# Attention and a gated feed-forward: the sum of e over the partitions by accumulating transfers

## The chip, the core and the metric

The kernel runs on one core of a Trainium2 chip. Its time is the device time of one execution in microseconds (us), the median of three runs. The engines of the core work side by side, each with its own queue of instructions in a fixed order, and wait for each other by semaphores: TensorE (PE) multiplies matrices, ScalarE (ACT) evaluates functions, VectorE (DVE) does elementwise work and sums, GpSimd (POOL) here issues transfers and clears a few tiles, and SyncE (SP) issues transfers. A transfer is issued from an engine's queue and carried out by 16 DMA engines that all queues share.

## The reference

Thirty-two heads (4 batches of 8) of 768 queries and keys, 64 numbers each. Queries and keys are hashed to six bits; a query sees only keys of its own bucket. The result, laid out as 3072 rows of 512, passes through a gated feed-forward with 2048 hidden columns.

```
q_bits = (einsum(q, proj) > 0); k_bits likewise          # 6 bits each
mask   = bucket(q)[..., :, None] == bucket(k)[..., None, :]
scores = where(mask, q @ k.T / sqrt(64), -1e9)
e      = exp(scores - max(scores))
x      = (e / (sum(e) + 1e-9)) @ v                       # to (3072, 512)
h      = x @ w_in
out    = (h * erf(softplus(h))) @ w_out
```

## The kernel before

Heads are worked two at a time: 16 pairs. In a pair each half of the queries (384 of 768) is a step h, so there are 32. Scores are held transposed, with 128 keys on the partitions and queries along the row, in six blocks per step for both heads of the pair: TensorE writes a block (`score`, L548), which adds a product of hash bits that pushes foreign buckets down and the product of q and k; ScalarE takes the exponential into `e_all` (L566), a ring of nine blocks; TensorE multiplies with v (`weigh`, L629).

The softmax needs, for every query, the sum of e over all keys. VectorE adds the six blocks of a step to one of 128 x 768 (`sum_keys`, L617). What remains is a sum over the 128 partitions. `divisor` (L664) does it on TensorE by four products with a block of ones; `keep_divisor` (L677) copies the result from PSUM. When both steps of a pair are there, `spread` and `gather` (L707, L714) take the 1536 sums through DRAM to 128 partitions, `invert` (L724 to L727) takes reciprocals, and `ungather`, `widen` (L732, L742) bring them back, repeated over 64 partitions. `normalise` (L750) multiplies, `send` stores x to DRAM.

Beside that the weights come in. They arrive as 64-bit numbers in 32 pieces of 128 x 512 (`fetch_weights`, L454, from GpSimd's queue but for the first two). VectorE and ScalarE turn each into 32 bits: `square_high` and `keep_normal` on ScalarE, `move_bits` (two instructions), `mask_bits` (two) and `add_rest` (two) on VectorE. In `add_rest` one instruction makes the rest from the low word (L522) and a second adds it to the top (L530). `presum_weights` (L771) forms sums of weight blocks that the feed-forward uses in place of some products.

GpSimd's queue also carries the hash bits of the pair after next: `leave_bits` (L846) writes signs to DRAM, `place_bits` (L855, two transfers) brings them to the rows where TensorE reads them. The second waits for the first to land, and the scores of that pair wait for both.

The order of all this is made by a planner, `arrange`: each operation has an engine, a cost, a rank, a list of operations that it follows, and `late`, the time after its end until another engine can use its result. The planner plays this through and writes each engine's instructions in the order it finds; on the chip each engine then keeps that order and waits where data are not there. In the planner `late` counts between engines only:

```
away = 0.0 if names[a].engine == op.engine else names[a].late     # L141
```

Attention and feed-forward are planned apart; the last pair's divisor is finished inside the feed-forward (`late`). The feed-forward works six blocks of 512 rows; it has transfers from GpSimd's queue that add to what stands in SBUF (`accum_op`, L1372), fifteen in all.

Of the kernel before, what the change touches and what calls it, by code (L numbers as in the profile page):

```python
# [193 lines left out]
def kernel(  # L194
# [219 lines left out]
    def attention():  # L414
        NS = NPAIR * 4
        with (
# [10 lines left out]
            def big(name):  # L427
# [49 lines left out]
            def move_bits(n):  # L477
                if n not in raws:
                    return
                high = raws[n][:, :, 1]  # L480
                top = raws[n, "top"] = cvt.tile([P, WP], I32, name="top", tag="top")
                nc.vector.tensor_scalar(
                    out=top,
                    in0=high,
                    scalar1=3,
                    scalar2=0x7FFFFFFF,
                    op0=ALU.logical_shift_left,
                    op1=ALU.bitwise_and,
                )
                nc.vector.scalar_tensor_tensor(  # L490
                    out=top,
                    in0=high,
                    scalar=SIGN,
                    in1=top,
                    op0=ALU.bitwise_and,
                    op1=ALU.bitwise_or,
                )

            def mask_bits(n):
                if n not in raws:  # L500
                    return
# [13 lines left out]

            def add_rest(n):
                if n not in raws:
                    return
                top, unit = raws.pop((n, "top")), raws.pop((n, "unit"))
                low = raws.pop(n)[:, :, 0]  # L520
                rest = cvt.tile([P, WP], F32, name="rest", tag="rest")
                nc.vector.scalar_tensor_tensor(  # L522
                    out=rest,
                    in0=low.bitcast(U32),
                    scalar=2.0**-52,
                    in1=unit[:, :].bitcast(F32),
                    op0=ALU.mult,
                    op1=ALU.mult,
                )
# [63 lines left out]
            def sum_keys(h, k):  # L593
                i, half = divmod(h, 2)
                d = pairs[i]
                if k == 0:
                    if h >= NH - 2:
                        if half:
                            room = blocks[1][:, :, :].rearrange("p k t -> p (k t)")[:, 0:S]
                        else:  # L600
                            room = load.tile([P, S], F32, name="q", tag="q")
                        d["sum", half] = room.rearrange("p (n a c) -> p n a c", n=1, a=2)
                    else:
                        d["sum", half] = wide_sums[h % 2]
                s = d["sum", half]
# [9 lines left out]

                into = s[:, 0:2, :, :] if where == 2 else s[:, where : where + 1, :, :]
                nc.vector.tensor_tensor(out=into, in0=term(one), in1=term(two), op=ALU.add)  # L617

# [18 lines left out]
            def home(i, what):  # L637

                if i < NPAIR - 1:
                    shape, bufs = {"x": (S, 3), "z": (HS, 1), "r": (S, 2)}[what]  # L640
                    return xst.tile([P, shape], F32, name=what, tag=what, bufs=bufs)
                rows = blocks[1][:, :, :].rearrange("p k t -> p (k t)")
# [47 lines left out]
            def leave_plain(i):  # L690
# [9 lines left out]
                )  # L700

            def spread(i):

# [25 lines left out]
            def ungather(i):  # L729
                d = pairs[i]  # L730
                rd = d["rd"] = dram.tile([2, 2, HS], F32, name="rd", tag="rd")
                nc.sync.dma_start(  # L732
                    out=rd.rearrange("h a c -> (h a c)").rearrange("(p c) -> p c", c=2 * S // P),
                    in_=d["zc"],
# [144 lines left out]
            for h in range(NH):  # L879
# [3 lines left out]
                if h % 2 and (h + 3) // 2 < NPAIR:  # L883
                    order.append(("bits", (h + 3) // 2))
                if h >= 1:
                    order.append(("divisor", h - 1))
                order += [("weigh", 2 * h), ("weigh", 2 * h + 1)]
            slots = []
            for what, n in order:
# [12 lines left out]
                else:  # L902
                    h = n // 2
                    after = (("exponential", n, GC - 1),)
                    if n % 2 == 0:
                        after += (("leave", h - 1), ("leave_plain", (h - 1) // 2))
                    pe(weigh, (n,), 2.02, after)
            sums_after = {}
            for h in range(NH):
# [16 lines left out]
            for h in range(NH):  # L926
                for k, (blocks_, _, _, where) in enumerate(sum_steps(h)):
                    after = tuple(("exponential", 2 * h + b // GC, b % GC) for b in blocks_)
                    after += (("sum_keys", h, k - 1), ("sum_keys", h - 1, last_sum(h - 1)))
                    if k == 0:  # L930
                        after += (("divisor", h - 2),)
# [13 lines left out]
            for h in range(NH):  # L945
                i = h // 2
                op(leave, (h,), "ACT", 0.48, (0, 2 * h, -2), (("weigh", 2 * h + 1), ("send", i - 3)))
                if h % 2 == 0:
                    op(leave_plain, (i,), "DVE", 0.15, (0, 2 * h, 0), (("weigh", 2 * h + 1),))
            for i in range(NPAIR):  # L950
# [40 lines left out]
                if i == NPAIR - 1:  # L991
                    continue
                op(spread, (i,), "SP", 0.4, (0, n, 0), (("keep_divisor", 2 * i + 1),), late=3.0)
                op(gather, (i,), "SP", 0.35, (0, n, 1), (("spread", i),), late=4.5)
                op(invert, (i,), "DVE", 0.4, (0, n + 8, 3), (("gather", i),))
                op(ungather, (i,), "SP", 0.35, (0, n, 2), (("invert", i),), late=3.0)
                op(
# [12 lines left out]
            for n in range(len(pieces)):  # L1010
# [13 lines left out]
                op(mask_bits, (n,), "DVE", 1.1, (2, n, 1), (("move_bits", n), ("keep_normal", n)), late=1.5)  # L1024
                op(add_rest, (n,), "DVE", 1.3, (2, n, 2), (("mask_bits", n),))
            for k in range(8):
                op(
                    presum_weights,
                    (k,),
                    "DVE",  # L1030
                    1.2,
                    (2, 31, k),
                    (("add_rest", 8 * (k // 4) + 7), ("presum_weights", k - 1)),
                )
            op(load_x, (0,), "SP", 1.1, (1, 0), (("send", JP - 1), ("start_pair", 10)), late=4.0)
# [748 lines left out]
```

## Time and profile before

| | |
|---|---|
| median of three runs | 911.17 us (909.92 to 911.47) |
| the profiled execution, its own time | 910.96 us |
| span of its trace, first to last instruction | 909.2 us |
| attention, to TensorE's first product of the feed-forward | 321.6 us |
| TensorE busy | 900.3 us |
| VectorE, ScalarE, GpSimd busy | 673.3, 571.9, 58.2 us |
| TensorE clock granted in the span (mean) | 0.999 |
| records of products with ones (L664) | 256, 0.33 us each, eight to a divisor |

Busy times of an engine are sums of its instructions; where one engine is busy all the time, the others' idle time costs nothing. In rows of instructions the first numbers are the start in the span and the duration, then engine, line, operation, and written tile <- read tiles with their shapes; brackets hold the idle time before an instruction and what ended it. A row of transfers holds their count, the size of one and the time from issue to landing. In rows by stretch of time the columns are PE, weight loads, DVE, ACT, POOL busy time, then the granted clock, the share of the DMA engines and GB/s.

### The profile page before, as it was taken

What the parts mean: (1) busy time and instruction counts of PE and PEld (TensorE: products, weight loads), DVE (VectorE), ACT (ScalarE), POOL (GpSimd) and SP (SyncE); (2) the same over time, 40 slices, a digit from 0 to 9 for tenths busy, and PEclk for the clock granted to TensorE, in tenths of its full rate; (3) what the DMA queues carried; (4) which work ended last, traced back from release to release, by engine and by line L of the source; (5) the groups of instructions that cost most, each with busy time, mean ns of one, the idle gap of its engine ahead of it and who ended that gap; (6) DMA issues with size and microseconds to landing.
All of it is one profiled execution on the core that took longest, in us unless ns stands there. A gap on an engine that the chain in (4) does not pass through costs nothing.

```text
span 909.2 us, 12885 instructions
## 1 busy us (share of the span) xinstructions
PE 900.3 (99%) x5016; PEld 661.9 (73%) x5016; DVE 673.3 (74%) x863; ACT 571.9 (63%) x824; POOL 58.2 (6%) x95
## 2 busy tenths in 40 slices
PE   9999999999999999999999999999999999999997
PEld 5444444444444478888888888888888888888886
DVE  5989999989999969986566556756776556655653
ACT  6878887888887849755555545555655555545520
POOL 0211111111121000000000001000100000000000
PEclk9999999999999999999999999999999999999999
DMA  8455677656574231111122114211321023101321
GB/s 203 130 162 148 169 176 189 187 141 165 157 194 136 59 123 64 38 45 70 52 65 82 35 47 105 81 36 47 87 99 35 35 58 94 35 32 52 69 70 50
DMA packets 65013, 86.83 MB, mean 96 GB/s; under 512 B 34348, under 2 KB 47500, under 8 KB 64944
## 3 DMA queue, kind: packets, MB, share of 16 engines
q1 hardware_dynamic: 56384, 63.81, 24.6%
q0 software_dynamic: 8112, 21.66, 8.6%
q8 instruction: 41, 0.67, 0.3%
q10 hardware_dynamic: 448, 0.46, 0.2%
q14 instruction: 28, 0.23, 0.1%
HBM read 64.67 MB, written 17.30 MB: 90 GB/s over the span
## 4 chain that ended last, share of the span: by engine, by line
PE 92%; issue 1%; DMA 1%; ACT 0%; POOL 0%; DVE 0%; DVEq 0%; ACTq 0%; POOLq 0%
PE M L1317 32%; PE X L1204 28%; PE st L548 14%; PE av L629 12%; PE M L1204 3%; PE z_ps L664 1%; PE bits L817 1%; DMA raw<-in_w_in_dram 0%; POOL both L855 0%; ACT e_all L566 0%; ACT keep L468 0%; DMA bd<-sg 0%; DVE u L1352 0%; ACT x L688 0%; DVEq L1727 0%
## 5 line engine op out<-in xcount | busy, mean ns | idle before, releaser
L1244 DVE SCALAR_TENSOR_TENSOR e<-w,e 128x1024 f32<-128x1024 f32 x144 | 173.8, 1221 | 8.9 <-ACT w L1238 4.2
L566 ACT ACTIVATE e_all<-st 128x768 f32<-128x768 f32 x192 | 150.9, 813 | 11.9 <-PE st L548 11.5
L1238 ACT ACTIVATE w<-h,cq 128x1024 f32<-128x1024 f32 x144 | 155.6, 1137 | 0.2 <-DVE e L1244 0.2
L548 PE MATMUL st<-q,k 64*128 64x384 f32 x768 | 155.0, 483 | 0.0
L1226 DVE TENSOR_TENSOR h<-X,h 128x512 f32<-128x512 f32 x65 | 44.8, 689 | 146.0 <-PE X L1204 145.8
L1317 PE MATMUL M<-w_out_sb,h 128*128 128x256 f32 x576 | 141.5, 379 | 0.0
L629 PE MATMUL av<-e_all,v 128*64 128x385 f32 (+1 forms) x768 | 131.1, 490 | 0.0
L1204 PE MATMUL X<-x,w_in_sb 128*128 128x256 f32 x512 | 121.0, 379 | 0.0
L1317 PEld LDWEIGHTS M<-w_out_sb,h 128*128 128x128 f32 x576 | 109.4, 190 | 14.9
L1222 ACT COPY h<-X 128x512 f32<-128x512 f32 x85 | 49.3, 580 | 112.4 <-PE X L1204 112.3
L1234 ACT ACTIVATE e<-h,cq 128x1024 f32<-128x1024 f32 x48 | 55.2, 1150 | 82.7 <-DVE h L1226 82.7
L1204 PEld LDWEIGHTS X<-x,w_in_sb 128*128 128x128 f32 x512 | 97.3, 190 | 13.2
L629 PEld LDWEIGHTS av<-e_all,v 128*64 128x64 f32 x768 | 52.4, 136 | 67.2 <-issue 65.2
L1317 PE MATMUL M<-wt,S 128*128 128x256 f32 x384 | 95.6, 379 | 0.0
L548 PEld LDWEIGHTS st<-q,k 64*128 64x128 f32 x768 | 68.2, 188 | 34.9 <-issue 34.2
L1204 PE MATMUL X<-x_sum,w_sum 128*128 128x256 f32 x344 | 81.3, 379 | 0.0
L1317 PEld LDWEIGHTS M<-wt,S 128*128 128x128 f32 x384 | 73.0, 190 | 9.9
L1204 PEld LDWEIGHTS X<-x_sum,w_sum 128*128 128x128 f32 x344 | 65.4, 190 | 8.9
L548 PE MATMUL st<-both 64*128 64x384 bf16 x384 | 62.9, 324 | 1.6 <-ACT e_all L566 1.4
L1259 DVE TENSOR_TENSOR h<-h,e 128x1024 f32<-128x1024 f32 x48 | 58.0, 1221 | 3.7 <-ACT e L1255 3.6
L1255 ACT ACTIVATE e<-e 128x1024 f32<-128x1024 f32 x48 | 50.4, 1054 | 7.8 <-DVE e L1244 7.4
L548 PEld LDWEIGHTS <-both 64*128 64x128 bf16 x384 | 19.5, 94 | 43.1 <-issue 21.2
(126 smaller groups left out, 1073.4 us busy)
## 6 DMA issues: line engine op xcount, KB each, us to landing
wt<-wt SPq DMA_DIRECT2D x24, 768.0 KB, 4.2
raw<-in_w_out_dram POOLq DMA_DIRECT2D x16, 512.0 KB, 4.6
raw<-in_w_in_dram POOLq DMA_DIRECT2D x14, 512.0 KB, 4.3
v<-in_v_dram SPq DMA_DIRECT2D x32, 192.0 KB, 4.8
xs<-x SPq DMA_DIRECT2D x16, 384.0 KB, 3.1
q<-in_qkT_dram SPq DMA_DIRECT2D x30, 192.0 KB, 4.2
k<-in_qkT_dram SPq DMA_DIRECT2D x30, 192.0 KB, 4.4
r<-rd SPq DMA_DIRECT2D x30, 192.0 KB, 3.4
```

Source lines behind the costliest of these rows:

```text
L548: nc.tensor.matmul(out=st[:, ab, 0:HS], lhsT=d["k" + src][rows, keys], rhs=d["q" + src][rows, cols], start=(part == 0), stop=(part == 1),)
L566: nc.scalar.activation(out=e[:, :, 0:HS], in_=st[:, :, 0:HS], func=AF.Exp, scale=scale)
L629: nc.tensor.matmul(out=d["av"][rows, 0:w], lhsT=d["v"][:, g * GC + c, rows], rhs=e[:, ab, 0:w], start=(g == 0 and c == 0), stop=(g == 1 an ...
L1204: nc.tensor.matmul(out=d[where][:, u, :], lhsT=a[:, kc, f : f + P], rhs=b[:, kc, :], start=(first and u == 0 and kc == 0), stop=(last and ...
L1222: nc.scalar.copy(out=quarter(p, q), in_=st[p][where])
L1226: nc.vector.tensor_tensor(out=h, in0=st[p][where], in1=h, op=ALU.add)
L1234: nc.scalar.activation(out=s, in_=unit(p, v), func=AF.Sigmoid, bias=cq[:, n : n + 1])
L1238: nc.scalar.activation(out=q, in_=unit(p, v), func=AF.Sigmoid, scale=GATE_S[j][0], bias=cq[:, j : j + 1])
L1244: nc.vector.scalar_tensor_tensor(out=s, in0=st[p].pop(("q", v, j)), scalar=GATE_S[j][2], in1=s, op0=ALU.add, op1=ALU.mult,)
L1255: nc.scalar.activation(out=s, in_=s, func=AF.Tanh, scale=GATE_LEAD)
L1259: nc.vector.tensor_tensor(out=h, in0=h, in1=st[p].pop(("s", v)), op=ALU.mult)
L1317: nc.tensor.matmul(out=banks[name][:, sub, :], lhsT=a[:, u, sub * P : (sub + 1) * P], rhs=b[:, u, :], start=(c == 0 and k == 0), stop=(c = ...
```

## The change

For 14 of the 16 pairs (`FOLDED`) the products with ones and their copies are left out. The last addition of `sum_keys` writes its 128 x 768 into half of a row block of 128 x 1536 that holds both steps of the pair (`pair_sums`, two of them, used in turn). Four transfers from GpSimd's queue then add the lower half of the rows to the upper: 64 rows to 64, 32 to 32, 16 to 16, 8 to 8 (`fold`). Eight rows go to DRAM and come back as 64 partitions x 8 x 24; VectorE adds the eight and inverts. The last two pairs keep the old form.

For the weights, the second instruction of `add_rest` is replaced by an accumulating transfer of 128 x 512 (`complete_weights`): the top is formed where the weights will lie, and the rest is added there. `unit` gets two buffers; the order of `presum_weights` is new, with two of them after the last use of `w_sum` as a row block. `x` has four buffers in place of three.

```diff
+    FOLDS = 4
+            FOLDED = NPAIR - 2
+            pair_sums = [
+                t.rearrange("p a b -> p (a b)")[:, 0 : 2 * S]
+                for t in (blocks[1][:, :, :], w_sum[:, 2, :, :])
+            ]
...
-                top = raws[n, "top"] = cvt.tile([P, WP], I32, name="top", tag="top")
+                top = raws[n, "top"] = pieces[n][0].bitcast(I32)
...
-                unit = raws[n, "unit"] = cvt.tile([P, WP], I32, name="unit", tag="unit")
+                unit = raws[n, "unit"] = cvt.tile([P, WP], I32, name="unit", tag="unit", bufs=2)
...
-                nc.vector.tensor_tensor(
-                    out=pieces[n][0], in0=top[:, :].bitcast(F32), in1=rest, op=ALU.add
+
+            def complete_weights(n):
+
+                if (n, "unit") not in raws:
+                    return
+                nc.gpsimd.dma_start(
+                    out=pieces[n][0],
+                    in_=raws.pop((n, "unit"))[:, :].bitcast(F32),
+                    accum_op=ALU.add,
                 )
...
+                if i < FOLDED and k == last_sum(h):
+                    into = pair_sums[i % 2][:, half * S : (half + 1) * S].rearrange(
+                        "p (n a c) -> p n a c", n=1, a=2
+                    )
...
+            def fold(i, k):
+
+                n = P >> (k + 1)
+                s = pair_sums[i % 2]
+                nc.gpsimd.dma_start(out=s[0:n, :], in_=s[n : 2 * n, :], accum_op=ALU.add)
+
+            ROWS = P >> FOLDS
+
+            def spread_folded(i):
+
+                zf = pairs[i]["zf"] = dram.tile([ROWS, 2 * S], F32, name="zf", tag="zf")
+                nc.sync.dma_start(out=zf, in_=pair_sums[i % 2][0:ROWS, :])
+
+            def gather_folded(i):
+                d = pairs[i]
+                zr = d["zr"] = small.tile([D, ROWS, 2 * S // D], F32, name="zr", tag="zr", bufs=2)
+                nc.sync.dma_start(
+                    out=zr, in_=d.pop("zf").rearrange("r (p c) -> p r c", c=2 * S // D)
+                )
+
+            def invert_folded(i):
+                d = pairs[i]
+                zc = d["zc"] = small.tile([D, 2 * S // D], F32, name="zc2", tag="zc2")
+                nc.vector.tensor_reduce(
+                    out=zc, in_=d.pop("zr").rearrange("p r c -> p c r"), axis=AX.X, op=ALU.add
+                )
+                nc.vector.tensor_scalar(
+                    out=zc, in0=zc, scalar1=S * EPS, scalar2=None, op0=ALU.add
+                )
+                nc.vector.reciprocal(out=zc, in_=zc)
...
-                if h >= 1:
+                if h - 1 >= 2 * FOLDED:
                     order.append(("divisor", h - 1))
...
+                    if k == last_sum(h) and i_of(h) < FOLDED:
+                        after += (("spread_folded", i_of(h) - 2),)
...
-            for h in range(NH - 1):
+            for h in range(2 * FOLDED, NH - 1):
...
+                if i < FOLDED:
+                    for k in range(FOLDS):
+                        before = ("fold", i, k - 1) if k else ("sum_keys", 2 * i + 1, last_sum(2 * i + 1))
+                        op(fold, (i, k), "POOL", 0.9, (0, n, 4 + k), (before,), late=4.0)
+                    op(spread_folded, (i,), "SP", 0.4, (0, n, 0), (("fold", i, FOLDS - 1),), late=3.0)
+                    op(gather_folded, (i,), "SP", 0.35, (0, n, 1), (("spread_folded", i),), late=4.5)
+                    inverse = invert_folded
+                    op(inverse, (i,), "DVE", 0.7, (0, n + 8, 3), (("gather_folded", i),))
...
-                op(add_rest, (n,), "DVE", 1.3, (2, n, 2), (("mask_bits", n),))
...
+                op(add_rest, (n,), "DVE", 0.7, (2, n, 2), (("mask_bits", n), ("complete_weights", n - 2)))
+                op(complete_weights, (n,), "POOL", 0.9, (0, n, 1), (("add_rest", n),), late=4.5)
```

More of the change, by code (lines that the diff above doesn't have):

```diff
@@ L518, in add_rest @@
                     return
-                top, unit = raws.pop((n, "top")), raws.pop((n, "unit"))
+                raws.pop((n, "top"))
+                unit = raws[n, "unit"][:, :].bitcast(F32)
                 low = raws.pop(n)[:, :, 0]
-                rest = cvt.tile([P, WP], F32, name="rest", tag="rest")
                 nc.vector.scalar_tensor_tensor(
-                    out=rest,
+                    out=unit,
                     in0=low.bitcast(U32),
                     scalar=2.0**-52,
-                    in1=unit[:, :].bitcast(F32),
+                    in1=unit,
                     op0=ALU.mult,
@@ L603, in sum_keys @@
                     else:
-                        d["sum", half] = wide_sums[h % 2]
+                        d["sum", half] = wide_sums[h % 2 if i >= FOLDED else 0]
                 s = d["sum", half]
@@ L639, in home @@
                 if i < NPAIR - 1:
-                    shape, bufs = {"x": (S, 3), "z": (HS, 1), "r": (S, 2)}[what]
-                    return xst.tile([P, shape], F32, name=what, tag=what, bufs=bufs)
+                    if what == "z":
+                        return x_sum[:, :, :, :].rearrange("p a b c -> p (a b c)")[:, S : S + HS]
+                    return xst.tile([P, S], F32, name=what, tag=what, bufs={"x": 4, "r": 2}[what])
                 rows = blocks[1][:, :, :].rearrange("p k t -> p (k t)")
@@ L732, in ungather @@
                 nc.sync.dma_start(
-                    out=rd.rearrange("h a c -> (h a c)").rearrange("(p c) -> p c", c=2 * S // P),
+                    out=rd.rearrange("h a c -> (h a c)").rearrange(
+                        "(p c) -> p c", c=2 * S // (D if i < FOLDED else P)
+                    ),
                     in_=d["zc"],
@@ L907, in attention, with i_of @@
                     pe(weigh, (n,), 2.02, after)
+            def i_of(h):
+                return h // 2
             sums_after = {}
@@ L930, in attention @@
                     if k == 0:
-                        after += (("divisor", h - 2),)
+                        if h == NH - 3:
+                            after += (("spread_folded", FOLDED - 2),)
+                        if h - 2 >= 2 * FOLDED:
+                            after += (("divisor", h - 2),)
                         if h == NH - 2:
                             after += (("measure", NPAIR - 3, 0, 1),)
+                    if k == last_sum(h) and i_of(h) < FOLDED:
+                        after += (("spread_folded", i_of(h) - 2),)
                     op(sum_keys, (h, k), "DVE", 1.72 if where == 2 else 0.92, (1, 2 * h + 1, k), after)
-            for h in range(NH - 1):
+            for h in range(2 * FOLDED, NH - 1):
                 i = h // 2
@@ L946, in attention @@
                 i = h // 2
-                op(leave, (h,), "ACT", 0.48, (0, 2 * h, -2), (("weigh", 2 * h + 1), ("send", i - 3)))
+                op(leave, (h,), "ACT", 0.48, (0, 2 * h, -2), (("weigh", 2 * h + 1), ("send", i - 4)))
                 if h % 2 == 0:
@@ L992, in attention @@
                     continue
[L993 to L996, printed above, removed]
+                if i < FOLDED:
[6 more added lines that the diff above has]
+                    op(inverse, (i,), "DVE", 0.7, (0, n + 8, 3), (("gather_folded", i),))
+                else:
+                    op(spread, (i,), "SP", 0.4, (0, n, 0), (("keep_divisor", 2 * i + 1),), late=3.0)
+                    op(gather, (i,), "SP", 0.35, (0, n, 1), (("spread", i),), late=4.5)
+                    inverse = invert
+                    op(inverse, (i,), "DVE", 0.4, (0, n + 8, 3), (("gather", i),))
+                op(ungather, (i,), "SP", 0.35, (0, n, 2), ((inverse.__name__, i),), late=3.0)
                 op(
@@ L1024, in attention @@
                 op(mask_bits, (n,), "DVE", 1.1, (2, n, 1), (("move_bits", n), ("keep_normal", n)), late=1.5)
-                op(add_rest, (n,), "DVE", 1.3, (2, n, 2), (("mask_bits", n),))
[L1026 to L1034, printed above, removed]
+                op(add_rest, (n,), "DVE", 0.7, (2, n, 2), (("mask_bits", n), ("complete_weights", n - 2)))
+                op(complete_weights, (n,), "POOL", 0.9, (0, n, 1), (("add_rest", n),), late=4.5)
+            before = ()
+            for n, k in enumerate((0, 1, 2, 4, 5, 6, 3, 7)):
+                after = tuple(("complete_weights", 8 * (k // 4) + m) for m in range(8))
+                if k % 4 == 3:
+                    after += (("spread_folded", FOLDED - 1),)
+                op(presum_weights, (k,), "DVE", 1.2, (2, 31, n), after + before)
+                before = (("presum_weights", k),)
             op(load_x, (0,), "SP", 1.1, (1, 0), (("send", JP - 1), ("start_pair", 10)), late=4.0)
```

## The prediction

> **What bounds the kernel now.** I read the page's busy times, slices and chain first, to find the engine that sets the end.
>
> ```profile
> PE 900.3 (99%) x5016; PEld 661.9 (73%) x5016; DVE 673.3 (74%) x863; ACT 571.9 (63%) x824; POOL 58.2 (6%) x95
> PE   9999999999999999999999999999999999999997
> DVE  5989999989999969986566556756776556655653
> PE 92%; issue 1%; DMA 1%; ACT 0%; POOL 0%; DVE 0%; DVEq 0%; ACTq 0%; POOLq 0%
> ```
>
> TensorE never rests. Attention is the first third (to 321.6 us, where the chain turns to L1204), and there VectorE is nearly full as well. Next, TensorE's own instructions over one divisor (start, duration, both in us), and two pieces of the chain for the period of a pair.
>
> ```profile
> 134.88 0.53 PE L664 MATMUL z_ps<-x,ones 128*32 128x192 f32 x8
> 135.34 4.10 PE L629 MATMUL av<-e_all,v 128*64 128x385 f32 x24
> 141.81 0.33 PE L548 MATMUL st<-both 64*128 64x384 bf16 x2
> ```
>
> ```profile
> 139.45 4.95 PE st L548 x36
> 158.98 4.95 PE st L548 x36
> ```
>
> A divisor takes 135.34 - 134.88 = 0.46 us of TensorE, and a pair 158.98 - 139.45 = 19.5. The row at 141.81 is the first score of a pair that needs that pair's bits: three score blocks after the scores resume at 139.4. The third view is GpSimd's queue beside the sums that end on VectorE.
>
> ```profile
> 147.95 0.55 POOL L846 DMA_DIRECT2D bd<-sg  x1 [5.11 <-DVE sg L836]
> 152.21 1.15 POOL L855 DMA_DIRECT2D both<-bd  x2 [3.72 <-PE st L548]
> ...
> 128.18 0.96 DVE L617 TENSOR_TENSOR x<-x 128x768 f32<-128x768 f32 x1
> 146.34 0.96 DVE L617 TENSOR_TENSOR x<-x 128x768 f32<-128x768 f32 x1
> 140.41 3.23 ACT L566 ACTIVATE e_all<-st 128x768 f32<-128x768 f32 x4 [0.44 <-PE st L548]
> ```
>
> GpSimd stood 3.72 us idle between two transfers of which the second reads what the first wrote: a dependent transfer holds this queue. Last, what transfers take from issue to landing (count, KB each, median us), and the share of the DMA engines in a stretch of attention.
>
> ```profile
> bd<-sg POOLq DMA_DIRECT2D x14, 96.0 KB, 3.5
> both<-bd POOLq DMA_DIRECT2D x28, 21.0 KB, 3.9
> proj_in<-in_proj_dram POOLq DMA_DIRECT2D x1, 6.0 KB, 3.1
> row<-in_bucket_dram POOLq DMA_DIRECT2D x1, 0.5 KB, 3.0
> u<-part POOLq DMA_DIRECT2D x10, 256.0 KB, 4.7
> zc<-zd SPq DMA_DIRECT2D x16, 6.0 KB, 1.6
> v<-in_v_dram SPq DMA_DIRECT2D x32, 192.0 KB, 4.8
> ```
>
> ```profile
> DMA to landing us min/median/max: 3.8/4.7/5.2
> ```
>
> ```profile
> 100.00:150.00 50.00, 50.00 (x374) 23.25 (x372) 48.12 (x68) 41.47 (x78) 6.79 (x12) 1.00 0.58 151
> ```
>
> The row of least, middle and longest is of the accumulating transfers of the second half of the kernel (L1372), the same kind that the change uses: none has landed in under 3.8 us, and even half a KB takes 3.0.
>
> **What is removed.** 28 of 32 divisors leave TensorE: 28 x 0.46 = 12.9 us of a full engine. With them go 28 copies on ScalarE (0.32 each, 9 us) and 32 adds of 128x512 on VectorE (0.69 each, 22 us). Those engines are not the bound, so I price both at nothing; they would only count if TensorE had been waiting for them. On VectorE 14 reductions come in (64 x 192 numbers, some 0.3 each, 4 us), inside what the adds free.
>
> **What is added on GpSimd's queue.** For each of 14 pairs four accumulating steps, each reading what the last wrote, so each waits there for a landing; for each of 32 weight pieces one more transfer of 256 KB, which nothing waits for soon. The planner counts a landing only for a successor on another engine (line 141), so it lays the four steps back to back, 0.9 us each. In the program's order, ten of the fourteen transfers of bits (pairs 2 to 5, 7, 9, 10, 12, 13, 15) stand behind all four steps of the pair two before. For the other four (6, 8, 11, 14) the bits go first.
>
> Price of a step: I draw a line through 6 KB at 3.1 and 256 KB at 4.5 (the middle of 3.8 and 5.2), 0.0056 us a KB. The steps move 384, 192, 96 and 48 KB: 5.2, 4.1, 3.6 and 3.3 us, 16.2 together. Bounds: 3.0 each (the least landing of the queue) and 5.2 each (the longest of the accumulating row).
>
> The Trainium skill (DMA: Bandwidth & Descriptors, "Two DMAs through the same engine are not ordered") has the issuing engine wait for the first transfer's semaphore before the dependent one goes out; the 3.72 us of idle above agree, and this rule speaks against a chain. The same page ("Anatomy of one DMA") fits 2.0 us plus bytes over 436e3 to such a transfer; that gives 2.9, 2.5, 2.2 and 2.1 us for the steps, and by it alone the sum below would end near 938. It gives 2.6 us for the 256 KB that the trace shows at 4.7, so the row decides.
>
> **The ten pairs whose bits stand behind the steps.** After the pair's last sum: 5.2 + 4.1 + 3.6 = 12.9 for three landings, 0.9 for the fourth's issue (it is not waited for here), 4.3 from L846 to L855 in the row above (152.21 - 147.95; 4.0 is usual over the stretch, and I take 4.0), 0.6 for the first half of L855, 3.9 for the second to land: 22.3 us. Time that TensorE gives: from the end of the sum at 129.1 to the score at 141.8 is 12.7; one pair later from 147.3 to 161.4 (158.98 and three blocks of 0.81) 14.1; less a divisor, 13.0 in the mean. TensorE stands 22.3 - 13.0 = 9.3 us, ten times: 93 us. Behind the waiting GpSimd stand also the weights' completing and fetching, for which VectorE would wait next; I count that as lying in the same stand.
>
> **The other four.** There the sum's own way back is late: VectorE's queue holds the inversion at a fixed place, and whatever is behind waits. The way: 16.2 for the steps, 3.4 to write to DRAM (in the old form the spread at 135.83 and the gather at 139.27), and a gather of 48 KB in pieces of 96 bytes, which I put at 2.3 between 1.6 for 6 KB and 4.8 for 192 KB; 21.9, and 0 to 4 us more because these steps now stand behind the bits, so 2: 23.9. In VectorE's new order 11.9 us of work (by the rows' durations) stand between the pair's sum and the inversion, which is 12.9 where VectorE is 92% busy (48.1 of 50 us in the stretch shown, less the adds that go). The stop of 11.0 reaches TensorE through ScalarE: blocks freed by a sum at 137.7 are written again at 140.4 (2.8 us of room), and TensorE runs three scores ahead (2.4). 11.0 - 5.2 = 5.8, four times: 23 us. In the ten pairs above this stop falls into TensorE's own stand and isn't counted again.
>
> **The sum.** The profiled execution took 910.96 (span 909.2 and 1.8 around it; the median of the runs is 911.17, 0.2 more). 910.96 - 12.9 + 93 + 23 = 1014. With every step at 3.0: 10 x 5.4 + 4 x 1.6 = 60, 958. With every step at 5.2: 10 x 12.0 + 4 x 10.4 = 162, 1060. The second part of the kernel is as it was; two weight sums moved to the end of attention may add 2 us, which I leave in the range.
>
> **Rivals.**
> *The queue doesn't hold (faster).* If the steps cost only their 0.9 us of issue, nothing of the above happens and the divisors are gained: 910.96 - 12.9 = 898. For it: TensorE at 99%, and room on GpSimd (6% busy). It decides where three landings take no more than 13.0 - 9.4 = 3.6 us, 1.2 each; against it, no transfer of this queue landed in under 3.0. Chance 0.04 (0.01 more that both sides cancel).
> *Short steps, and the inversion hidden.* Steps at 3.0 and the four inversions covered by the room that VectorE gained: 910.96 - 12.9 + 54 = 952. For it: the adds taken off VectorE. Against: the 3.8 of the accumulating row. Chance 0.10.
> *The DMA engines fill.* Between 100 and 150 us they are busy for 0.58 (the last but one number of that row), 11.3 us of a pair's 19.5. New traffic per pair is 720 KB of steps and 512 KB of weights; at 1.4 us per 250 KB that is 6.9 us more, 18.2 of the 18.6 that a pair would have. Then landings stretch; at half as much again the steps take 24.3, the ten stands 15.8 each, the four 13.9: 910.96 - 12.9 + 158 + 56 = 1112. Against: TensorE's own stands thin the traffic out to two thirds. Chance 0.11.
>
> **Numbers.** My forecast has 0.74, and its own range, 958 to 1060, is that of the unknown price of a step. With the 952 of the short steps inside, the range is 948 to 1062. Slower by over 0.2% (1.8 us, about what a measurement of this kernel tells from no change) 0.95, within it 0.01, faster 0.04.
>
> **What would show it.** In the profile after: TensorE no longer at 9 in the attention slices; idle time of TensorE before the score products of 60 to 120 us, most of it put to GpSimd's or the DMA's placing of bits; on GpSimd a wait of 2 to 5 us before each step but the first; the pair's period near 27 us instead of 19.5; VectorE idle before the reduction. The second part should keep its length. I am wrong if the steps land in about 1 us, if GpSimd issues a step without waiting for the last, or if the periods stay under 19 us.

## The result and the profile after

The changed kernel takes 1074.73 us (median, 1073.11 to 1078.64) against 910.72 us of the kernel before beside it: 1.181 times as long, interval 1.177 to 1.184. The profiled execution has a span of 1073.0 us against 909.2. Attention now ends at 483.6 us instead of 321.6; the feed-forward behind it takes 589 us against 588. The page's busy times, slices (PEclk is the clock granted to TensorE, in tenths) and chain:

```profile
PE 927.4 (86%) x4792; PEld 675.2 (63%) x4792; DVE 661.5 (62%) x845; ACT 566.1 (53%) x796; POOL 134.7 (13%) x183
PE   9677666694867568599999999999999999999997
PEclk9888889798888789889999999999999999999999
DMA  8566665777675776543110231032013211201311
PE 55%; DVE 1%; issue 1%; DMA 0%; POOL 0%; ACT 0%; DVEq 0%
```

TensorE is no longer full in most of the first 18 slices, and its clock falls there. It has fewer instructions and yet is busy for 27 us longer: 12.9 us of divisors went, so 40 us came from the products that stayed, at a lower clock. Idle it is for 137 us more. 27 + 137 makes the 164 us. The view of the waits (engine, tile and line <- what ended the wait: us in total, times, longest) says who let it stand:

```profile
PE st L561 <- DMA both<-bd: 93.1, 12, 13.0
POOL x L724 <- DMA x<-x: 85.6, 21, 7.5
POOL w_sum L724 <- DMA w_sum<-w_sum: 85.6, 21, 7.3
DVE zc L743 <- DMA zr<-zf: 74.6, 14, 12.9
DVE w_out_sb L488 <- DMA raw<-in_w_out_dram: 43.8, 7, 7.9
PE st L561 <- ACT e_all L579: 43.6, 9, 8.7
```

The accumulating transfers of `fold` are called steps from here on. TensorE waits for the bits, GpSimd before every step but the first of a pair (21 + 21 waits = 14 pairs x 3), and VectorE 14 times before the reduction. The timeline of GpSimd, then of TensorE, then of VectorE, over a pair whose bits stand behind the steps and the pair after it, whose bits go first:

```profile
186.88 0.87 POOL L724 DMA_DIRECT2D w_sum<-w_sum  x1 [9.09 <-DVE w_sum L634]
192.28 0.78 POOL L724 DMA_DIRECT2D w_sum<-w_sum  x1 [4.53 <-DMA w_sum<-w_sum]
198.94 0.76 POOL L724 DMA_DIRECT2D w_sum<-w_sum  x1 [5.88 <-DMA w_sum<-w_sum]
...
203.09 0.83 POOL L724 DMA_DIRECT2D w_sum<-w_sum  x1 [1.91 <-DMA w_sum<-w_sum]
203.62 0.87 POOL L897 DMA_DIRECT2D bd<-sg  x1
207.53 1.18 POOL L906 DMA_DIRECT2D both<-bd  x2 [3.03 <-issue]
...
220.83 1.16 POOL L906 DMA_DIRECT2D both<-bd  x2 [3.52 <-PE st L561]
221.97 0.94 POOL L724 DMA_DIRECT2D x<-x  x1
...
248.30 0.85 POOL L724 DMA_DIRECT2D w_sum<-w_sum  x1 [9.39 <-DVE w_sum L634]
...
209.77 1.00 PE L561 MATMUL st<-both 64*128 64x384 bf16 x2 [9.36 <-DMA both<-bd]
210.28 1.78 PE L561 MATMUL st<-q,k 64*128 64x384 f32 x4
...
216.49 0.96 DVE L634 TENSOR_TENSOR x<-x_sum 128x768 f32<-128x768 f32 x1
...
246.05 0.61 DVE L743 TENSOR_REDUCE zc<-zr 64x24 f32<-64x192 f32 x1 [9.38 <-DMA zr<-zf]
...
247.12 0.89 DVE L634 TENSOR_TENSOR w_sum<-x_sum 128x768 f32<-128x768 f32 x1
```

In the first pair the steps begin at 186.88 and the score they hold up comes at 209.77, 22.9 us later, close to the 22.3 forecast. The second pair is the surprise. Its sum ends at 217.45; its steps stand behind bits that wait for TensorE to release their rows, and start at 221.97; the eight rows are back at 246.05, and VectorE stood 9.38 us for them. The last sum of the next pair is 1.07 us behind that reduction in VectorE's queue. So the way back of one pair's sum holds up the sum of the next, and with it the next steps (248.30, after 9.39 us of waiting for that sum). That is one closed chain: steps, bits or reduction, sum, steps. From pair 1 to pair 13 the pairs' last sums start at 58.46 and 435.84: 377.4 us for 12 pairs, 31.4 each instead of 19.5.

Transfers (count, KB each, median us to landing): the steps, to be held against the forecast's 5.2, 4.1, 3.6 and 3.3, the bits, and the accumulating transfers of the weights (`unit`):

```profile
w_in_sb<-unit POOLq DMA_DIRECT2D x16, 256.0 KB, 4.5
w_out_sb<-unit POOLq DMA_DIRECT2D x16, 256.0 KB, 3.9
x<-x POOLq DMA_DIRECT2D x7, 384.0 KB, 7.1
w_sum<-w_sum POOLq DMA_DIRECT2D x7, 384.0 KB, 5.2
x<-x POOLq DMA_DIRECT2D x7, 192.0 KB, 4.8
bd<-sg POOLq DMA_DIRECT2D x14, 96.0 KB, 3.4
w_sum<-w_sum POOLq DMA_DIRECT2D x7, 192.0 KB, 6.4
x<-x POOLq DMA_DIRECT2D x7, 96.0 KB, 3.5
w_sum<-w_sum POOLq DMA_DIRECT2D x7, 96.0 KB, 3.6
both<-bd POOLq DMA_DIRECT2D x28, 21.0 KB, 2.2
x<-x POOLq DMA_DIRECT2D x7, 48.0 KB, 3.7
```

### The profile page after: what moved, and what is told of

Same layout as the page of the kernel before. It is cut to its first block, busy times and chain, and to the rows that moved or that the text cites. A ratio compares the mean times of both kernels' runs of the same rounds, so it can differ in the third digit from the quotient of the medians.

```text
span 1073.0 us, 12532 instructions
## 1 busy us (share of the span) xinstructions
PE 927.4 (86%) x4792; PEld 675.2 (63%) x4792; DVE 661.5 (62%) x845; ACT 566.1 (53%) x796; POOL 134.7 (13%) x183
## 4 chain that ended last, share of the span: by engine, by line
PE 55%; DVE 1%; issue 1%; DMA 0%; POOL 0%; ACT 0%; DVEq 0%
PE M L1385 27%; PE X L1272 24%; PE M L1272 2%; PE st L561 1%; PE av L646 1%; DVE wt L1357 0%; DVE w_sum L822 0%; DMA both<-bd 0%; DVE x_sum L341 0%; DVE x L634 0%; DVE w_out_sb L1357 0%; PE z_ps L682 0%; DVE h L1294 0%; DVE x L801 0%; DMA bd<-sg 0%
## 5 line engine op out<-in xcount | busy, mean ns | idle before, releaser
L561 PE MATMUL st<-both 64*128 64x384 bf16 x384 | 78.3, 365 | 137.1 <-DMA both<-bd 93.1
L561 PE MATMUL st<-q,k 64*128 64x384 f32 x768 | 184.6, 553 | 0.0
L579 ACT ACTIVATE e_all<-st 128x768 f32<-128x768 f32 x192 | 148.7, 813 | 62.2 <-PE st L561 61.2
L561 PEld LDWEIGHTS <-both 64*128 64x128 bf16 x384 | 26.2, 102 | 192.9 <-issue 88.2
L561 PEld LDWEIGHTS st<-q,k 64*128 64x128 f32 x768 | 82.7, 217 | 34.4 <-issue 33.4
L474 ACT ACTIVATE keep<-raw 128x512 f32<-128x512 f32 x32 | 21.6, 674 | 117.2 <-DMA raw<-in_w_in_dram 51.1
L1440 POOL DMA_DIRECT2D u<-part x10 | 8.7, 869 | 511.7 <-DVE S L1342 479.2
```

Of the source, the lines that this page charges most:

```text
L474: nc.scalar.activation(out=sq, in_=high.bitcast(F32), func=AF.Square)
L561: nc.tensor.matmul(out=st[:, ab, 0:HS], lhsT=d["k" + src][rows, keys], rhs=d["q" + src][rows, cols], start=(part == 0), stop=(part == 1),)
L579: nc.scalar.activation(out=e[:, :, 0:HS], in_=st[:, :, 0:HS], func=AF.Exp, scale=scale)
L1440: nc.gpsimd.dma_start(out=outs[WAYS[k]], in_=outs.pop(("part", k)), accum_op=ALU.add)
```

## The experiments

Times are medians, ratios are against the kernel before run beside them (910.3 to 911.2 us). All edits are to the changed kernel unless another is named.

**Which part of the change: the weights or the steps?** `weights_only` and `weights_alone` set `FOLDED = 0`: the weights' rest still goes by transfers, every pair keeps its divisor. In `weights_only` the copies of the divisor (`z`) lay in a tile that VectorE's sums use; `weights_alone` gives them their own. `folds_only` keeps the steps and gives the weights' addition back to VectorE.

```diff
-            FOLDED = NPAIR - 2
+            FOLDED = 0                       # weights_only, weights_alone
...
+                    shape, bufs = {"x": (S, 3), "z": (HS, 1), "r": (S, 2)}[what]   # weights_alone
...
+                nc.vector.tensor_tensor(out=pieces[n][0], in0=pieces[n][0], in1=unit, op=ALU.add)   # folds_only
```

> All 16 pairs sum over the partitions by products with ones again; only the rest of the weights is added by accumulating transfers (32 of 256 KB). Theory (GpSimd's queue is held by steps that wait for the landing of the step before): nothing waits soon for these transfers, TensorE is full again, so 905 to 913 us, no difference to the 911 of before. Rival (the DMA engines fill): these transfers are 8.4 of the 18.7 MB that the change adds, 45%, so about 911 + 0.45 x 164 = 985.

> As weights_only, but the divisors' copies have a tile of their own again, as in the kernel before (in weights_only they lay where VectorE's sums lie, and ScalarE waited 36 us for VectorE at that copy). Theory: TensorE is full again and the weights' transfers are waited for by nobody, 908 to 914. Rival (the added traffic alone costs time): 8.4 MB more on the DMA engines lengthen the landing of the bits, 920 or more.

> The 14 pairs are summed by accumulating steps as in the changed kernel; the rest of the weights is added by VectorE again. Theory: the chain on GpSimd's queue is there as before, so 1055 to 1090 us. Rival (the DMA engines fill): 45% of the new traffic is gone, so about 1000.

`weights_only`: 921.55 us, 1.0125 (1.0103 to 1.0146), 9 us above its theory. ScalarE stood 36.4 us before its copies into that tile, so this run doesn't price the weights. `weights_alone`: 914.97, 1.0044 (1.0027 to 1.0060), 1 us above the 908 to 914 expected: 32 transfers for 22 us of VectorE's additions cost 4 us, although the share of the DMA engines between 50 and 300 us rises from 0.61 to 0.77. `folds_only`: 1089.13, 1.1951 (1.1927 to 1.1975), as the theory had it; the waits of this run:

```profile
DVE zc L744 <- DMA zr<-zf: 149.5, 14, 15.6
PE st L562 <- DMA both<-bd: 123.6, 11, 16.3
```

The steps alone bring the whole loss and 14 us more. So the additions that the weights leave to transfers are a help here; that this is because VectorE is in the chain fits its longer wait for the reduction (149.5 us against 74.6), but isn't shown by itself.

**Does the wait between the steps do it?** In `apart` the four transfers of a pair have the same sizes and stand at the same places of the queue, but add into cleared rows in `w_out`'s place, so none waits for another, and the eight rows go out without waiting for them. Left out by this are the sums of the other 120 rows.

```diff
-                nc.gpsimd.dma_start(out=s[0:n, :], in_=s[n : 2 * n, :], accum_op=ALU.add)
+                nc.gpsimd.dma_start(
+                    out=w_out_sb[:, NF - 3 : NF, :].rearrange("p f c -> p (f c)")[P - 2 * n : P - n, :],
+                    in_=s[n : 2 * n, :], accum_op=ALU.add)
```

> The four steps move the same rows and add as before, but each adds into rows of its own that nothing reads (in the last rows of w_out's place, cleared at the start), so none waits for the step before. Left out by this: the sums of the lower 120 rows never reach the upper 8. Theory (the waits in GpSimd's queue): the traffic costs little, attention ends near 311 us, 895 to 905 in all. Rival (traffic on the DMA engines): 1040 or more.

996.17 us, 1.0931 (1.0879 to 1.0983): 79 us come back and 85 don't. Neither theory had that. Timeline and transfers of this run:

```profile
151.60 2.46 POOL L725 DMA_DIRECT2D w_out_sb<-w_sum  x3 [9.73 <-DVE w_sum L635]
...
155.56 1.40 POOL L902 DMA_DIRECT2D bd<-sg  x1
170.32 1.18 POOL L911 DMA_DIRECT2D both<-bd  x2 [13.36 <-issue]
```

```profile
bd<-sg POOLq DMA_DIRECT2D x14, 96.0 KB, 10.4
```

The steps go out together, and the bits behind them then take 10.4 us to land instead of 3.4: 720 KB of steps and the weights' pieces are under way on the same queue and engines. The wait has moved from the queue into the transfer. A chain that waits at least leaves the way clear for what follows it.

**Is the lower clock a cause of its own?** `fill` gives TensorE 18 instructions that nobody reads (nine products of 512 columns) in front of each of the ten scores that wait.

```diff
+                if n % 4 == 0 and c == 0 and n // 4 in (2, 3, 4, 5, 7, 9, 10, 12, 13, 15):
+                    fill = bank("fill")
+                    for _ in range(9):
+                        nc.tensor.matmul(out=fill[0:D, :], lhsT=ones,
+                            rhs=ones[:, 0:1].broadcast_to([P, 512]), start=True, stop=True)
```

> The changed kernel, with nine idle products (64 rows out, 512 columns, an estimated 0.86 us each from 0.38 to 0.43 us per 256 columns in the trace) on TensorE before the first score of each of the ten pairs that wait for their bits, 7.7 us in stands of 8 to 13. If the lower clock after a stand (0.78 to 0.91 granted in attention) costs time of its own: the clock in attention rises above 0.92 and the time falls by 15 to 25 us, to 1048 to 1060. If GpSimd's chain alone sets the period: the clock rises and the time stays within 5 us of 1074.

1071.77 us, 1.1761 (1.1737 to 1.1784). By stretches (PE, weight loads, DVE, ACT, POOL busy, then clock, DMA share, GB/s), the changed kernel and then `fill`:

```profile
50.00:450.00 400.00, 277.98 (x1664) 131.14 (x1664) 226.33 (x301) 199.09 (x350) 105.14 (x143) 0.84 0.67 147
```

```profile
50.00:450.00 400.00, 331.53 (x1811) 144.54 (x1812) 225.82 (x301) 198.62 (x350) 103.88 (x142) 0.93 0.68 147
```

The clock rises from 0.84 to 0.93, and about 3 us come of it, hardly more than the runs differ among themselves. The chain through the steps keeps its length, so TensorE's quicker products only make it wait longer. The 40 us of slower products in the first account are a consequence, not a cause.

**Is it the order in GpSimd's queue?** The planner counts `late` between engines only. `plan_late` makes it count also where one transfer follows another in the same queue; `plan_steps` does so for the steps alone.

```diff
+LANDS = ("fold", "leave_bits", "spread", "spread_folded")     # plan_steps: ("fold",)
...
-                away = 0.0 if names[a].engine == op.engine else names[a].late
+                same = names[a].engine == op.engine and a[0] not in LANDS
+                away = 0.0 if same else names[a].late
```

> As plan_late, but only the steps' landing is counted in the same queue, not that of the bits' way out or the way to DRAM. Theory: the steps' 15 us of waiting per pair are the larger part, so 905 to 960; if the bits' own 4 us matter as much, above 985.

> The changed kernel, with one change in the planner: a step, the bits' way out and the way to DRAM count their landing also for a successor in the same queue, so the bits are laid ahead of steps whose landing would hold them and the inversion stands later on VectorE. The same instructions and the same traffic in another order. Theory (order in GpSimd's queue): most of the 164 us goes; with all stands gone 898, with landings of 10 us instead of 3.4 for the bits, as seen in the run with the steps apart, 920 to 950. Rival (the DMA engines can't carry the traffic at this pace): it stays above 985.

`plan_late`: 958.75 us, 1.0536 (1.0485 to 1.0587), 9 us above the theory's 950 and well under the rival's 985. `plan_steps`: 988.61, 1.0851 (1.0827 to 1.0876), so the other landings that `plan_late` counts, of the bits and of the ways to DRAM, matter too. GpSimd's timeline in `plan_late`:

```profile
145.42 0.86 POOL L728 DMA_DIRECT2D w_sum<-w_sum  x1 [2.19 <-DVE w_sum L638]
146.85 0.60 POOL L901 DMA_DIRECT2D bd<-sg  x1 [0.56 <-DVE sg L891]
151.30 0.86 POOL L545 DMA_DIRECT2D w_in_sb<-unit  x1 [3.85 <-DVE unit L532]
152.18 0.79 POOL L728 DMA_DIRECT2D w_sum<-w_sum  x1
153.33 1.23 POOL L910 DMA_DIRECT2D both<-bd  x2 [0.36 <-issue]
...
159.28 0.86 POOL L728 DMA_DIRECT2D w_sum<-w_sum  x1 [4.13 <-DMA w_sum<-w_sum]
```

The bits now go between the first and the second step, and the landing of the one covers the landing of the other. The steps are the same, the transfers too; the order is worth 116 of the 164 us. It isn't the order of GpSimd's queue alone: the same edit moves the reduction on VectorE. In the changed kernel it stands 1.1 to 5.5 us ahead of the next pair's last sum, in `plan_late` 10 to 22 us behind it (in `plan_steps` 6 to 20), so VectorE's part of the loop is broken there as well. 30 of the 116 us need the landings of the bits and the ways to DRAM; for the other 86 no run takes the two queues apart. From 74.13 to 326.31 us the first steps of 12 pairs are 22.9 us apart.

**Are the other 48 us the load of the DMA engines?** The queue's line on the page: packets, MB, share of the 16 engines' span, in `plan_late`.

```profile
q0 software_dynamic: 15408, 40.37, 21.0%
```

Before it was 21.66 MB at 8.6%. That is 201 us of 956 against 78 of 909: 123 us of all sixteen engines for 18.7 MB more. In `thin_late` each new transfer (steps and weights) moves half of its columns, in `thin_after` likewise with the changed kernel's own order; left out by this are the sums over the partitions of half of each row and the rest of half of the weights' columns.

```diff
-                nc.gpsimd.dma_start(out=s[0:n, :], in_=s[n : 2 * n, :], accum_op=ALU.add)
+                nc.gpsimd.dma_start(out=s[0:n, 0:S], in_=s[n : 2 * n, 0:S], accum_op=ALU.add)
...
+                    out=pieces[n][0][:, 0 : WP // 2],
+                    in_=raws.pop((n, "unit"))[:, 0 : WP // 2].bitcast(F32),
```

> plan_late with the same instructions in the same order, but every step and every transfer that completes weights moves half of its columns: 9.3 MB of new traffic instead of 18.7. Left out by this: the sums of the second step of each of the 14 pairs, and the rest of half of the weights' columns. Theory (what remains in plan_late, 48 us over the kernel before and 61 over what the divisors would give, is the DMA engines, busy for 0.89 of that stretch): 905 to 925. Rival (what remains is the number of landings that the queue waits for): 940 or more.

> The changed kernel in its own order with the same halving of columns (the same is left out). Theory (order first): each step still waits for a landing, of some 3.4 to 4.5 us instead of 3.6 to 6.4, so the ten stands shrink by about 4 us each and the four late inversions by as much: 1005 to 1035. Rival (traffic first): under 975.

912.82 us, 1.0028 (1.0014 to 1.0043), as the theory had it, and 980.37, 1.0771 (1.0743 to 1.0799), between theory and rival. But half the bytes also shorten the steps, so this doesn't tell load from length. For that the load of others was to be made lighter. First by reading v so that a partition takes six keys in a row (and k's columns with a stride of six to match), in the kernel before, in `plan_late` and in the changed kernel:

```diff
-                in_=v[b, 2 * j + ab].rearrange("(c p) d -> p c d", p=P),
+                in_=v[b, 2 * j + ab].rearrange("(p c) d -> p c d" if runs else "(c p) d -> p c d", p=P),
...
-                            lhsT=d["k" + src][rows, keys],
+                            lhsT=d["k" + src][rows, :].rearrange("p (r c) -> p c r", c=NC)[:, part_of, :],
```

> The kernel before, with v read so that a partition takes six keys in a row (pieces of 1536 bytes in place of 256) and the keys of a score block taken every sixth from k to match. A control for the next run. Theory: TensorE sets the end whatever the DMA engines do, so 908 to 914 if weights can be read every sixth column at no cost, and more if not; the DMA engines' share of 0.58 to 0.65 falls by 0.1 or more.

> plan_late with the same reading of v: all of the computation, all bytes, the same steps in the same order, but some 20000 packets of 256 bytes fewer from the other queue. Theory (what remains in plan_late is the load of the DMA engines): it falls from 959 to between 900 and 920, as the run with half of the new bytes did (913); under 910 it would beat both kernels. Rival (what remains belongs to the accumulating transfers themselves, which landed later for their own bytes): above 940.

> The changed kernel in its own order with the same reading of v. Theory (order and load both): between the 980 of the run with half of the new bytes and the 1074 of the changed kernel, about 1020. Rival (order alone): within 10 us of 1074.

923.13 us, 1.0131 (1.0115 to 1.0146); 961.43, 1.0557 (1.0539 to 1.0575); 1077.03, 1.1823 (1.1802 to 1.1845). The last two lie where their rivals put them, but tell nothing of the load: the number of packets stayed (76844 in `late_v` as in `plan_late`), and so did the share of the engines, 0.90 against 0.91. What they show is the price of the stride: a weight load of k took 307 ns instead of 188. Then by leaving work out: from the fourth pair a sixth of v is loaded, from the third piece half of each raw weight, into fixed tiles, and the steps are untouched (`late_light` in `plan_late`'s order, `after_light` in the changed kernel's; `late_thin_light` has both cuts).

```diff
+                out=d["v"][:, 0 : 1 if vs and i > 2 else NC, ab * D : ab * D + D],
...
+                    w = WP if n < 2 else WP // 2
+                        out=raws[n][:, 0:w, :].rearrange("p c two -> p (c two)"),
```

> plan_late with the steps and their bytes untouched; other transfers are cut instead: v's move one of six key blocks from the fourth pair on (16600 packets of 256 bytes fewer), those of the raw weights half of their columns from the third piece on (7.9 MB fewer). Left out by this: five sixths of v in 13 pairs and half of the weights' columns, in whose place older numbers stand. By the packets' own times in plan_late this takes some 50 us of the 16 engines' time off, as much as halving the new bytes did. Theory (the engines' load as a whole): near that run's 913, 905 to 925. Rival (the length of the accumulating transfers themselves): above 940.

> The changed kernel in its own order with v and the raw weights cut as in late_light (the same is left out), the steps untouched. Theory (order first, the engines' load second): 1074 falls by 40 to 70 us, less than the 94 of halving the new bytes since the steps keep their length: 1005 to 1035. Rival (only the steps' own length counts in this order): 1060 or more.

> Both cuts together, half of the new bytes and the lighter other transfers, in the planner's order that counts landings (what each leaves out is left out). Theory: with the engines' load at the level of the kernel before, the 12.9 us of the 28 divisors come out at last: 897 to 904. Rival (the gain isn't there, something else on TensorE's way takes it): 908 to 914.

| | changed order | landings counted |
|---|---|---|
| all bytes | 1074.73 | 958.75 |
| others lighter | 1050.96, 1.1539 (1.1515 to 1.1562) | 924.38, 1.0158 (1.0135 to 1.0181) |
| new transfers at half | 980.37 | 912.82 |
| both | not run | 901.08, 0.9893 (0.9876 to 0.9909) |

`late_light` and `late_thin_light` came as their theories had it; `after_light` fell between the two. In the right order lighter transfers of *others* bring back 34 of the 48 us with the steps as they are, so most of the rest is the load. TensorE's wait for the bits falls with it, in `plan_late` and then in `late_light`:

```profile
PE st L565 <- DMA both<-bd: 30.5, 12, 5.0
```

```profile
PE st L571 <- DMA both<-bd: 11.6, 7, 3.4
```

The rows of 50 to 300 us, in `plan_late`, `late_light` and `late_thin_light`:

```profile
50.00:300.00 250.00, 218.30 (x1390) 102.41 (x1388) 187.03 (x249) 168.78 (x293) 87.86 (x119) 0.95 0.91 201
```

```profile
50.00:300.00 250.00, 237.16 (x1580) 110.69 (x1578) 214.10 (x285) 191.56 (x334) 100.46 (x138) 0.99 0.85 186
```

```profile
50.00:300.00 250.00, 250.00 (x1718) 115.93 (x1716) 233.25 (x311) 207.22 (x362) 106.64 (x142) 1.00 0.67 159
```

At a share of 0.91 TensorE stands for 32 of 250 us, at 0.85 for 13, at 0.67 never; there the divisors' time appears at last, 10 of the 12.9 us. The share alone doesn't give the stand: in `thin_late` it is 0.84 with 5 us, in the two runs below 0.81 (`plan_folds`) and 0.83 (`six`) with 25 and 22. The Trainium skill (DMA: Bandwidth & Descriptors, "Issuing engines are not separate DMA queues") has the transfers of all issuing engines run on the same 16 DMA engines; the 34 us that lighter transfers of others give back agree, though the run doesn't tell SyncE's (v) from GpSimd's own (the raw weights).

**Fewer steps.** Can a part of the change keep the gain? `half` folds seven pairs in the changed order; `plan_folds` is `folds_only` in `plan_late`'s order; `six` folds six pairs in that order, with one buffer for `unit` and `z` in its own tile.

```diff
+            FOLDED = NPAIR // 2 - 1          # half
+            FOLDED = 6                       # six
...
+                op(add_rest, (n,), "DVE", 1.3, (2, n, 2), (("mask_bits", n),))          # plan_folds
```

> Only the first 7 pairs are summed by steps, the other 9 by products with ones; the weights as in the changed kernel. Theory (a stand per pair whose bits are behind steps): five of the ten such places remain (bits of pairs 2, 3, 4, 5 and 7) and one or two of the four late inversions, so about half of the 164: 985 to 1005. Rival (one bottleneck that is full, like the DMA engines over all of attention): less than a third remains, under 965, since the average load falls under its limit.

> The steps in the planner's order that counts landings, the rest of the weights added by VectorE: 10.3 of the 18.7 MB of new traffic, and 22 us more on VectorE, which was busy for 0.96 in the kernel before. Theory (DMA engines): 915 to 935. If it isn't below 950, the steps and not the weights' transfers fill the engines, or VectorE is the bound.

> Six pairs by steps, ten by products with ones, all weights completed by transfers, the planner counting landings: 12.8 of the 18.7 MB, 12 of the 28 divisors saved (5.5 us). Theory: TensorE sets the end again nearly everywhere, 905 to 918; a gain over the kernel before only if the steps' landings stay under 6 us.

`half`: 1006.53, 1.1048 (1.1016 to 1.1080), 1.5 us above its theory. It has the shared tile of `weights_only`, and the sum of its first pair with a divisor may write into a row block that is still being folded, so it is no clean point. `plan_folds`: 941.79, 1.0347 (1.0319 to 1.0375), and `six`: 942.10, 1.0357 (1.0340 to 1.0374); both were expected below 935 and 918. In `six` the share of the DMA engines in the first 200 us, where its folded pairs lie, is 0.86, the bits take 7.9 us to land and the steps of 192 KB 7.5 to 8.0. Six pairs by steps cost more than their divisors there. Late bits alone don't explain it: of TensorE's idle time before the scores in `six` only 4.6 us are put to the bits and 18.1 to `e_all`; the cause stays open. No version found that computes everything is faster than the kernel before; the nearest, `weights_alone`, has no steps.

## Why the prediction was wrong in size

**What bounds, and the direction: right.** The rivals "the queue doesn't hold" (898) and "short steps" (952) fell: the shortest step landed in 3.46 us, and GpSimd stood 171 us between steps. Two readings behind it were wrong and did no harm. The 3.72 us of idle were ended by TensorE, as the row's bracket says; the transfer before had landed 0.6 us earlier (four other waits of the kernel before do name that landing, 13.9 us in all). And 3.0 us is the least of the medians, not "the least landing of the queue": single transfers of 96 and of 21 KB had landed in 1.9 and 2.1 us.

**The ten pairs: mechanism right, two terms mis-sized.** From the first step to the score nine of them (all but pair 0's) take 23.9 us in the mean (19.8 to 27.0), 22.3 forecast. Inside it two errors go against each other: three landings took 16.7, not 12.9, and the fourth step with the bits 7.2, not 9.4. In these nine the first three steps landed in 6.1, 5.9 and 3.7 us in the mean, not 5.2, 4.1 and 3.6, and 1.0 us more passed before the next went out; the longest step took 8.1, where the bound was 5.2. That price came from accumulating transfers of the second part, where the DMA engines are busy for 0.2 of the time, while the steps ran at 0.67. But load isn't shown to be the only reason: at the same 0.67 the accumulating transfers of the weights, 256 KB in 128 rows, landed in 4.5 and 3.9 us in the median, no later than those of the second part. The steps move fewer and longer rows, and no run separates shape from load. The other term is "I count that as lying in the same stand". From the score to the next sum 5.6 us were left (19.5 - 0.9 - 13.0); 7.3 were measured (the mean of the eight with another folded pair before and behind them). VectorE comes late there; its waits for raw weights behind GpSimd (74 us over the run) and for the reduction fit that, and 0.6 us of it goes when `fill` raises the clock. From sum to sum such a pair takes 32.0 us (mean of eight), not 27.9: 41 us over ten.

**The other four: the step that failed.** "11.0 - 5.2 = 5.8": VectorE's stop was 8.2 us, not 11.0 (the mean of 9.38, 9.38, 5.23 and 8.86): the way back took 28.3 us, not 23.9, and VectorE came to the reduction after 20.1 us, not 12.9. (The 92% behind the 11.0 come out at 91, 0.2 us less.) But the error lies in the 5.2 of room subtracted, which is the room of ScalarE and TensorE. In all four the next pair's last sum stands 1.1 us behind the reduction on VectorE, so the stop passes in full into the next pair's steps, and the room never counts. And the steps behind the bits came 3.3 to 4.8 us late where the bits waited for TensorE, not 2. Such a pair takes 30.4 us, not 24.4 (19.5 - 0.9 + 5.8): 24 us over four. With nothing subtracted it would have been 29.6. 41 + 24 = 65, against the 61 that the forecast of 1014 missed; neither alone would have taken the time out of the range (1055 and 1038).

**The stands agree by luck.** The 93.1 us that the waits put to the bits are the forecast's 93, but one of the ten is put to `e_all`; the ten stands together have 101 us, those of the four pairs 35 (23 forecast). The products' lower clock, which the forecast doesn't name, is worth some 3 us (`fill`).

**"The DMA engines fill": named, priced for the wrong place.** At 1112 it was to stretch the landings by half. In the changed kernel the stands themselves keep the share at 0.67 and three landings went up from 12.9 to 16.7, by 0.3 and not by half. The load becomes the bound only when the order is mended, at 0.91. The rival's price was short as well: 1.4 us per 250 KB is a difference of landings, not time of the engines. By the engine time measured in `plan_late` (6.6 us per MB) a pair's 1.26 MB take 8.3 us, not 6.9, and 11.3 + 8.3 = 19.6 is more than the 18.6 that a pair would have.

**Signs foretold.** Idle TensorE before the scores 137 us (60 to 120 forecast), periods 31.4 (27), waits of 2 to 5 us before each step (up to 7.5), the second part unchanged (589 to 588): directions right, sizes too small: a closed chain was priced as separate stands, and the steps landed later.

**What stays open.** Whether the 13 us that `late_light` leaves of the 48 are still load or the steps' length; how the 116 us divide between GpSimd's order and VectorE's; why `six` is slow; and what the bits would gain from a queue of their own, which was not tried.

## What to carry to other kernels

A chain of dependent transfers in one queue costs its landings to everything behind it, so tell the planner of landings within a queue too, and let other transfers go between the links: here the orders that this gave were worth 116 of 164 us. When a delay is hidden by room, ask whose queue stands behind it: two stands that feed each other's start make a loop, and then its whole length is the period. Price a transfer from others of its shape and at the load at which it will run, and count the engine time that it takes from others.

## What was not expected of the hardware

An accumulating transfer's landing isn't a matter of its size alone: 256 KB in 128 rows landed in 4.5 us in the second part (share 0.2) and in 3.9 to 4.5 in attention (0.67), while 192 KB in 32 rows took 4.8 to 6.4 at 0.67, and 7.5 to 8.0 at 0.86 (`six`). Per MB the new traffic took 6.6 us of all sixteen engines (123 us for 18.7 MB), what the queue carried before 3.6 (78 for 21.66). A transfer of 96 KB on a queue full of large ones took 10.4 us instead of 3.4 (`apart`, share 0.80); at a higher share but with fewer ahead of it in the queue 6.7 (`plan_late`, 0.91).

After a stand of 9.36 us four records of the score's products took 1.78 us instead of 0.81. In the changed kernel's attention the first products kept their pace after stands of up to 2.1 us (0.32 us for the first record) and lost it after those of 3.3 us and more (0.47 to 0.50). The Trainium skill (TensorE: Matmul & The Clock Gate, "HAM oscillation — how this bites in real kernels") warns of gaps over about 3.4 us for this reason; the rows agree, and yet it cost some 3 us here (`fill`), since TensorE wasn't what set the period.

A weight load whose 128 columns lie six numbers apart took 307 ns instead of 188 (`before_v`):

```profile
L548 PEld LDWEIGHTS st<-q,k 64*128 64x128 f32 x768 | 101.4, 307 | 31.0 <-issue 30.7
```
